# Powers of an exponential table computed directly, wider products, merged transfers and a halved inverse step in a DFT and long-convolution kernel

## The chip, the cores and the metric

The kernel runs on one core of one Trainium2 chip. The metric is the device time of one execution in microseconds (us). Lower is better.

## What is computed

Two independent parts whose results stand side by side in the output:

```python
# A: Fourier mixing, x is 2048 x 512
a = x @ dft_hid_re.T;  b = x @ dft_hid_im.T
ya = dft_seq_re @ a - dft_seq_im @ b
# B: diagonal state space layer as a long convolution, u is 2048 x 512, N = 128 states
dt = exp(log_dt);  A = -exp(log_A_real) + 1j * A_imag;  C = (C_real + 1j * C_imag) * dt
K[d, l] = 2 * real(sum_n C[d, n] * exp(A[d, n] * dt[d] * l))      # l = 0..2047
yb = irfft(rfft(u, 4096) * rfft(K, 4096))[:2048] + u * D_skip
out = concat(ya, yb)
```

All data are float32, and float32 accuracy is kept.

## The kernel before

The program is written by a planner (`Plan`): each piece of work is a generator that yields the engine it needs next and an assumed duration, and the planner, when the kernel is built, picks at each step the piece that can start first on its engine, with an urgency to break ties. What it picks is emitted at once. So each engine has a fixed order of instructions, and on the chip each engine takes its own in that order and waits wherever an operand isn't there.

**First part (`Fnet`).** Each product of two float32 tiles is three matmuls on a high and a low half (`hi`, `lo`). There are 12 groups: 8 named `("s", t, c)` with 16 row tiles each, 4 named `("p", t)` with 8. A row tile meets 4 column tiles `d`, so it gives 12 matmuls of 128 x 512, and the whole part gives 1920, all at L366. They are the *stream*, lowest in urgency, and fill TensorE wherever nothing else is ready. A row tile is loaded to `raw`, then split by one ScalarE copy to `hi` (L221) and one VectorE subtraction to `lo` (L225). Some pieces ("soft" ones) are split by two GpSimd transfers and one ScalarE copy instead. `evacuate` copies finished accumulators out; the last one (`d == 3` of the last group) is copied in two halves, by ScalarE (L382) and VectorE (L385).

**Second part (`Ssm`).** The kernel K is made from tables of powers. There are 16 blocks of 32 channels (`CHUNK`). For each block:

- `seed_args` (L636) makes the arguments of the powers 1, 2, 4, ..., 1024 of exp(A dt), 11 x 32 numbers for each row, and takes exponential, sine and cosine on ScalarE; `seeds` multiplies them to complex seeds `cs` (L675).
- `tables1` builds 32 outer powers `t1`, `tables2` 64 inner powers `t2`, by doubling: `mul` (L605) is a VectorE product with a seed, `add` (L614) combines real and imaginary parts, even powers come from squares (ScalarE L621, VectorE L628 and L634). Powers 3 and 5 to 7 of `t2` are two such products, of 128 and 384 elements for each row.
- `taps` (L801) sums over the states on TensorE: 64 calls of a 128 x 32 weight with 64 columns moving (float32 calls show as two matmuls each in the profile).

Every second block goes through `stage1_k` (L832), the first step of a Fourier transform in two steps; `stage1_u` (L890) is the same for u. Both go to DRAM and come back transposed. Then, for each quarter `h` of the channels and each of 4 parts `q`, `product` makes the second step for u and K (L992, 32 calls of 64 x 32 tiles with 256 columns), copies both out of PSUM on ScalarE (L1006), multiplies them on VectorE (L1009 to L1022), and makes the first inverse step with the matrix `ia` (L1029, 16 calls). The result is copied to `z` (L1044) and stored to `zs` in DRAM (L1053). When a quarter's four parts are stored, `inverse` runs twice for it: it loads half of `zs` as `zl` (L1073), makes the second inverse step with the matrix `ib` (L1078, 16 calls of a 128 x 64 weight with 128 columns moving), copies it out (two ScalarE copies, L1084) and stores 512 KB of the output (L1087).

The knobs that the change touches stand in these lines:

```python
LATE = 1, 1, 3, 1
...
CHUNK, FIRST, JOIN = 32, 128, 0
RAWS, DEPTH, STAGED, AHEAD = 7, 4, 4, 3
```

`LATE` is the urgency of a quarter's product copies, `RAWS` and `DEPTH` the numbers of buffers for `raw` and for `hi`/`lo`, `JOIN` the number of quarters whose first inverse step may share a TensorE block with `taps` (none).

## Time and profile before

| what | value |
|---|---|
| median of 3 runs | 583.82 us (583.13 to 583.96) |
| the profiled execution | 582.56 us |
| its span, first to last instruction | 580.8 us |
| TensorE (PE) matmuls busy | 571.1 us |
| VectorE (DVE) busy | 512.5 us |
| ScalarE (ACT) busy | 371.2 us |
| GpSimd (POOL) busy | 40.3 us |
| queue of SP, share of the 16 DMA engines' time | 66.7% |

The span is what the profile shows; the rest of an execution's time lies around it. "PEld" is TensorE's weight load, which overlaps the matmuls. Matmuls are pipelined: a stream matmul is listed with about 0.39 us, though the next one starts after 0.23, so what a run of them costs is read from starts, not from durations.

### The profile page before, as it was taken

What the parts mean: (1) busy time and instruction counts of PE and PEld (TensorE: products, weight loads), DVE (VectorE), ACT (ScalarE), POOL (GpSimd) and SP (SyncE); (2) the same over time, 40 slices, a digit from 0 to 9 for tenths busy, and PEclk for the clock granted to TensorE, in tenths of its full rate; (3) what the DMA queues carried; (4) which work ended last, traced back from release to release, by engine and by line L of the source; (5) the groups of instructions that cost most, each with busy time, mean ns of one, the idle gap of its engine ahead of it and who ended that gap; (6) DMA issues with size and microseconds to landing.
All of it is one profiled execution on the core that took longest, in us unless ns stands there. A gap on an engine that the chain in (4) does not pass through costs nothing.

```text
span 580.8 us, 15376 instructions
## 1 busy us (share of the span) xinstructions
PE 571.1 (98%) x6150; PEld 436.1 (75%) x6150; DVE 512.5 (88%) x911; ACT 371.2 (64%) x729; POOL 40.3 (7%) x60
## 2 busy tenths in 40 slices
PE   8999999999999999999999999999999999999996
PEld 6877777788777777778877777777687777776685
DVE  6999999999999999999999999999989999346410
ACT  4779665763777595768568585945588744445522
POOL 0000000000100000100000001001100000000000
PEclk9999999999999999999999999999999999999999
DMA  8999999986469767876797887479989995789564
GB/s 248 327 372 263 280 294 276 285 262 170 133 159 239 207 171 218 205 180 207 207 222 190 237 216 226 125 186 296 243 280 262 243 282 184 209 251 303 169 195 144
DMA packets 147831, 133.10 MB, mean 229 GB/s; under 512 B 47280, under 2 KB 107312, under 8 KB 147504
## 3 DMA queue, kind: packets, MB, share of 16 engines
q1 hardware_dynamic: 139408, 117.05, 66.7%
q0 software_dynamic: 8064, 14.68, 12.6%
q8 instruction: 48, 0.79, 0.6%
q10 hardware_dynamic: 288, 0.39, 0.2%
q14 instruction: 23, 0.19, 0.1%
HBM read 89.36 MB, written 42.73 MB: 227 GB/s over the span
## 4 chain that ended last, share of the span: by engine, by line
PE 70%; DVE 23%; issue 4%; DMA 2%; SPq 0%; ACT 0%; DVEq 0%; ACTq 0%
PE acc L366 55%; DVE prod L605 8%; DVE t L614 4%; PE f L992 4%; PE f L801 3%; DVE lo L225 3%; PE f L1029 3%; PE f L1078 2%; PE f L890 2%; DVE t L634 1%; PE f L832 1%; DVE z L1009 1%; DVE cs L675 1%; DMA zl<-zs 1%; DVE uk L1011 1%
## 5 line engine op out<-in xcount | busy, mean ns | idle before, releaser
L366 PE MATMUL acc<-hi,x_hi 128*128 128x512 f32 x640 | 258.2, 403 | 0.3 <-ACT hi L221 0.3
L366 PE MATMUL acc<-lo,x_hi 128*128 128x512 f32 x640 | 250.2, 391 | 0.0
L366 PE MATMUL acc<-hi,x_lo 128*128 128x512 f32 x640 | 249.7, 390 | 0.1
L605 DVE TENSOR_TENSOR prod<-t,cs 128x1024 f32<-128x1024 f32 (+4 forms) x192 | 163.1, 867 | 1.7 <-ACT t L723 0.6
L366 PEld LDWEIGHTS acc<-hi,x_hi 128*128 128x128 f32 x640 | 120.1, 188 | 49.8 <-issue 23.7
L366 PEld LDWEIGHTS acc<-hi,x_lo 128*128 128x128 f32 x640 | 120.3, 188 | 26.5 <-DVE x_lo L225 0.5
L366 PEld LDWEIGHTS acc<-lo,x_hi 128*128 128x128 f32 x640 | 120.3, 188 | 23.0 <-DVE lo L225 0.2
L221 ACT ACTIVATE hi<-raw 128x512 fp32r<-128x512 f32 x132 | 82.6, 627 | 64.0 <-PE acc L366 48.5
L225 DVE TENSOR_TENSOR lo<-raw,hi 128x512 fp32r<-128x512 f32 x132 | 90.1, 684 | 28.2 <-ACT hi L221 21.9
L614 DVE TENSOR_TENSOR t<-prod 128x512 f32<-128x512 f32 (+4 forms) x192 | 94.0, 511 | 1.0
L621 ACT ACTIVATE square<-t 128x256 f32<-128x256 f32 (+1 forms) x64 | 36.7, 573 | 31.0 <-DVE t L614 28.3
L320 POOL DMA_DIRECT2D lo<-in_sT x28 | 24.3, 868 | 214.1 <-ACT lo L318 33.8
L1006 ACT ACTIVATE uk<-f 128x1024 f32<-128x1024 f32 x32 | 31.1, 1017 | 11.8 <-PE f L992 11.8
L801 PEld LDWEIGHTS f<-t,t 128*32 128x32 f32 x2048 | 29.5, 110 | 7.9 <-issue 5.8
L801 PE MATMUL f<-t,t 128*32 128x64 f32 x2048 | 32.4, 220 | 1.9 <-issue 1.4
L389 ACT ACTIVATE y<-acc 128x512 f32<-128x512 f32 x47 | 28.0, 595 | 8.7 <-PE acc L366 8.6
L1009 DVE TENSOR_TENSOR z<-uk 128x512 f32<-128x512 f32 x32 | 21.9, 684 | 9.6 <-ACT uk L1006 7.4
L315 POOL DMA_DIRECT2D hi<-in_sT x28 | 16.2, 577 | 189.4 <-PE acc L366 147.0
L1044 ACT ACTIVATE z<-f 128x512 f32<-128x512 f32 x32 | 17.7, 592 | 13.3 <-PE f L1029 13.3
L634 DVE TENSOR_TENSOR t<-square 128x128 f32<-128x128 f32 (+1 forms) x64 | 24.6, 385 | 0.0
L992 PE MATMUL f<-xt,w 64*32 64x256 f32 x768 | 23.5, 379 | 0.0
L1011 DVE TENSOR_TENSOR uk<-uk 128x512 f32<-128x512 f32 x32 | 22.1, 690 | 0.9
(94 smaller groups left out, 490.7 us busy)
## 6 DMA issues: line engine op xcount, KB each, us to landing
raw<-in_sT SPq DMA_DIRECT2D x99, 256.0 KB, 5.4
p<-y SPq DMA_DIRECT2D x32, 256.0 KB, 3.2
xk<-xk_sb SPq DMA_DIRECT2D x32, 256.0 KB, 5.2
zs<-z SPq DMA_DIRECT2D x32, 256.0 KB, 3.3
zl<-zs SPq DMA_DIRECT2D x16, 512.0 KB, 5.0
raw<-p SPq DMA_DIRECT2D x32, 256.0 KB, 4.4
hi<-in_sT POOLq DMA_DIRECT2D x28, 256.0 KB, 4.6
lo<-in_sT POOLq DMA_DIRECT2D x28, 256.0 KB, 4.9
```

Source lines behind the costliest of these rows:

```text
L221: self.nc.scalar.activation(hi, src, AF.Copy)
L225: self.nc.vector.tensor_tensor(lo, src, hi.bitcast(F32), op=OP.subtract)
L366: nc.tensor.matmul(acc[d], l[:, cols], r, start=k == 0 and n == 0, stop=k == len(items) - 1 and n == 2)
L389: self.nc.scalar.activation(y, ps, AF.Copy, scale=-1.0 if g[2] == 1 else 1.0)
L605: self.nc.vector.tensor_tensor(p.rearrange("p k d c m -> p k (d c) m"), src.rearrange("p d c l -> p (d c) l")[:, None, :, rows].to_broadca ...
L614: self.nc.vector.tensor_tensor(dst[:, :, :, rows], p[:, 0], p[:, 1, :, ::-1], op=OP.add)
L621: self.nc.scalar.activation(sq, t[:, :, :, m // 2:m], AF.Square)
L634: self.nc.vector.tensor_tensor(t[:, :, 0, m:2 * m:2], box[0][:, :, 0], box[0][:, :, 1], op=OP.subtract)
L801: nc.tensor.matmul(ps[32 * j:32 * j + 32, i], t1[:, d, c], t2[:, d, c], start=c == 0, stop=c == 1, tile_position=(0, 32 * j))
L992: nc.tensor.matmul(got[r][1][32 * xx:32 * xx + 32, g, 256 * c:256 * c + 256], self.w2[rows, 2 * q + r, xx, 32 * c:32 * c + 32], xt[rows].r ...
L1006: a.activation(uk[:, r].rearrange("p g c n d -> p g (c n d)"), p, AF.Copy)
L1011: v.tensor_tensor(t[:, r], t[:, r], u[:, r, :, ::-1], op=OP.mult)
```

## The change

- **Powers 3, 5, 6, 7 directly.** The seed tile grows from 11 to 15 columns of 32. Four more ScalarE copies make 3, 5, 6 and 7 times the argument, and exponential, sine and cosine take them with the rest. One VectorE product of 256 elements makes a tile `ex` from them, and three ScalarE copies put it into `t2`. The two VectorE products and two sums that made these powers go.
- **Wide products.** For `h < 3` the two VectorE multiplications of a product run over both halves at once (1024 elements) after both ScalarE copies, not over each half (512) after its own.
- **Merged transfers.** The loads of `xt` and the store of `z` are one transfer where they were two (the tile of `h == 3` excepted, which lies in four buffers).
- **Halved second inverse step** for `h >= HALVED`, 2 (that is, 2 and 3): `inverse2`. The matrix `ia` gets a second version with another phase for `q >= 2`. `zl` is loaded as two halves of rows beside each other, one by SP's queue and one by GpSimd's; VectorE adds and subtracts them (two operations of 512 elements of each kind for each of the two `zl` tiles of a quarter); the step is then 32 calls of a 64 x 32 weight with 128 columns. The new matrix `ib2` is loaded after `zs` of `h == 1`.
- **Joining.** The second inverse step of `h < WAITS` (1), and what has waited, may share a TensorE block with `taps` or with a first inverse step (`late`).
- **The last copy** of the first part goes to two tiles, VectorE's first, and the stores of the last group are issued without a planned transfer slot.
- **The planner** gets 0.15 more slack ahead of TensorE, new durations for some pieces, `LATE = 3, 3, 3, 1`, `RAWS, DEPTH = 5, 5`; the set of soft pieces is written out, with the same members.

The core of the diff:

```diff
-LATE = 1, 1, 3, 1
+SLACK = 0.15
+LATE = 3, 3, 3, 1
...
                 if r[0] != p[5]:
-                    p[0] += HOP
+                    p[0] += HOP + (SLACK if r[0] == "pe" else 0.0)
...
         if g == self.groups[-1] and d == 3:
...
+            yield self.ys
+            y2 = self.pool.tile([128, DM], F32, name="y", bufs=STAGED)
+            yield "dve", dve(256)
+            self.nc.vector.tensor_copy(y2[:, 256:], ps[:, 256:])
             yield "act", act(256)
             self.nc.scalar.activation(y[:, :256], ps[:, :256], AF.Copy)
-            self.nc.sync.dma_start(out[:, :256], y[:, :256])
-            yield "dve", dve(256)
-            self.nc.vector.tensor_copy(y[:, 256:], ps[:, 256:])
-            self.nc.scalar.dma_start(out[:, 256:], y[:, 256:])
+            self.nc.sync.dma_start(out[:, 256:], y2[:, 256:])
+            self.nc.scalar.dma_start(out[:, :256], y[:, :256])
             return
...
-        s = self.tab.tile([128, 3, 11, CHUNK], F32, name="seed")
+        s = self.tab.tile([128, 3, 15, CHUNK], F32, name="seed")
...
+        for j, m in enumerate((3, 5, 6, 7)):
+            a.activation(args[:, :, j], args[:, :, 4], AF.Copy, scale=float(m))
...
+        ex = self.tab.tile([128, 2, 4, CHUNK], F32, name="ex", bufs=2)
+        yield "dve", dve(8 * CHUNK), *APART
+        self.nc.vector.tensor_tensor(ex, s[:, 1:3, :4], s[:, 0:1, :4].to_broadcast([128, 2, 4, CHUNK]), op=OP.mult)
...
-            p = yield from self.mul("prod2", t, slice(1, 2), cs[:, :, 1])
-            yield from self.add(p, t, slice(3, 4))
-            p = yield from self.mul("prod2", t, slice(1, 4), cs[:, :, 2])
-            yield from self.add(p, t, slice(5, 8))
+            ex = self.ex.pop(n)
+            yield "act", act(2 * CHUNK)
+            a.activation(t[:, :, :, 3].rearrange("p d c -> p c d"), ex[:, :, 0], AF.Copy)
+            for c in range(2):
+                yield "act", act(3 * CHUNK)
+                a.activation(t[:, :, c, 5:8].rearrange("p d j -> p j d"), ex[:, c, 1:], AF.Copy)
...
-            yield "dve", dve(512)
-            v.tensor_tensor(P[:, r], t[:, r], u[:, r], op=OP.mult)
-            yield "dve", dve(512), *APART
-            v.tensor_tensor(t[:, r], t[:, r], u[:, r, :, ::-1], op=OP.mult)
+            if h == 3:
+                yield from times(slice(r, r + 1), LAST)
...
         yield ready
+        if h < 3:
+            yield from times(slice(0, 2))
...
+    def inverse2(self, b, h, i, n):
+
+        nc, c = self.nc, n // 2
+        z = b.pool.tile([128, 2, c, PART], F32, name="zl", bufs=b.n)
+        view = self.zs[h].rearrange("(a s) c l d -> (s c) a l d", a=2)
+        yield "pool", ISSUE
+        for y, e in enumerate((nc.sync, nc.gpsimd)):
+            o = n * i + c * y
+            e.dma_start(z[64 * y:64 * y + 64], view[:, :, o:o + c])
+        yield "dma", load(64 * n, 270), FAST
+        t = b.pool.tile([128, c, PART], F32, name="zsum", bufs=b.n)
+        for w in range(0, c, 4):
+            m = slice(w, w + 4)
+            yield "dve", dve(512)
+            nc.vector.tensor_tensor(t[:, m], z[:, 0, m], z[:, 1, m], op=OP.add)
+            yield "dve", dve(512), *APART
+            nc.vector.tensor_tensor(z[:, 1, m], z[:, 0, m], z[:, 1, m], op=OP.subtract)
+        (k, ps), = yield from self.banks(1)
+        yield "pe", 1.06, None, 64
+        for o in range(0, c, 2):
+            for x in range(4):
+                for y in range(2):
+                    r, w = slice(64 * y, 64 * y + 64), o + x // 2
+                    nc.tensor.matmul(ps[32 * x:32 * x + 32, y, PART * (o // 2):PART * (o // 2) + PART],
+                                     self.ib2[r, c * i + w, x % 2], (t, z[:, 1])[x % 2][r, w], start=True, stop=True,
+                                     tile_position=(64 * y, 32 * x))
...
-RAWS, DEPTH, STAGED, AHEAD = 7, 4, 4, 3
+HALVED = 2
+RAWS, DEPTH, STAGED, AHEAD = 5, 5, 4, 3
+WAITS = 1
```

What the planner makes of it is read from the built order of both kernels. In the changed kernel the stream is L374, `taps` L833, the product L1025, the first inverse step L1069, the old second step L1172, the halved one L1145.

TensorE, the end of the program before: the second inverse steps of `h == 3` and the stream's last row tiles.

```order
L1078 MATMUL f1_7308<-zl_7272,ib_115 64x128 x16
L366 MATMUL acc_7191<-hi_7316,x_hi7_5770 128x512
L366 MATMUL acc_7191<-lo_7317,x_hi7_5770 128x512
L366 MATMUL acc_7191<-hi_7316,x_lo7_5771 128x512
L366 MATMUL acc_7220<-hi_7297,x_hi6_5733 128x512
L366 MATMUL acc_7220<-lo_7298,x_hi6_5733 128x512
L366 MATMUL acc_7220<-hi_7297,x_lo6_5734 128x512
L1078 MATMUL f0_7331<-zl_7273,ib_115 64x128 x16
L366 MATMUL acc_7220<-hi_7316,x_hi7_5770 128x512
L366 MATMUL acc_7220<-lo_7317,x_hi7_5770 128x512
```

After these rows 13 more stream matmuls follow, and the program ends with one. Now:

```order
L374 MATMUL acc_7205<-hi_7326,x_hi7_5650 128x512
L374 MATMUL acc_7205<-lo_7327,x_hi7_5650 128x512
L374 MATMUL acc_7205<-hi_7326,x_lo7_5651 128x512
L1145 MATMUL f1_7418<-zsum_7370,ib2_6657 32x128 x2
L1145 MATMUL f1_7418<-zl_7332,ib2_6657 32x128 x2
```

The first three rows are the last of the stream. Both halved steps of `h == 3`, 64 calls in all to `f1` and then `f0`, stand behind them, with 66 stream matmuls between the last first inverse step and them.

VectorE, the end of the program now (before, its last instruction is the copy L385, and only splits L225 stand ahead of it):

```order
L233 TENSOR_TENSOR lo_7288<-raw_7066,hi_7287 128x512
L233 TENSOR_TENSOR lo_7327<-raw_7083,hi_7326 128x512
L392 COPY y_7409<-acc_7205 128x256
L1136 TENSOR_TENSOR zsum_7370<-zl_7332 128x512
L1138 TENSOR_TENSOR zl_7332<-zl_7332 128x512
L1136 TENSOR_TENSOR zsum_7370<-zl_7332 128x512
L1138 TENSOR_TENSOR zl_7332<-zl_7332 128x512
```

The copy of the last accumulator `acc_7205`, which the stream's last matmul completes, stands ahead of the four operations of the first `zl` tile; four more, of `zl_7333`, follow.

VectorE, inside the tables, before (a block whose seeds are `cs_713`):

```order
L605 TENSOR_TENSOR prod2_1143<-t2_124,cs_713 128x128
L614 TENSOR_TENSOR t1_938<-prod_1126 128x32x16
L614 TENSOR_TENSOR t2_124<-prod2_1143 128x64
L605 TENSOR_TENSOR prod2_1173<-t2_124,cs_713 128x384
L225 TENSOR_TENSOR lo_1161<-raw_882,hi_1160 128x512
L902 TENSOR_TENSOR zl_249<-f0_1104,zl_249 128x512
L904 TENSOR_TENSOR zl_249<-f0_1104,zl_249 128x512
L614 TENSOR_TENSOR t2_124<-prod2_1173 128x64x3
```

and now the matching place of a block:

```order
L694 TENSOR_TENSOR cs_1442<-seed_1084 128x704
L699 TENSOR_TENSOR ex_1453<-seed_1084 128x256
L622 TENSOR_TENSOR prod_1451<-t1_1308,cs_1063 128x512
L233 TENSOR_TENSOR lo_1449<-raw_1366,hi_1448 128x512
L631 TENSOR_TENSOR t1_1308<-prod_1451 128x64x4
```

The four `prod2` instructions on `t2` are gone, and one product `ex` stands behind the seeds; the first `prod2` of a block is now the one of 512 elements. By the order, the stretch from the first `taps` to the last has 703 VectorE instructions before and 612 now.

## Rows read from the trace of the kernel before

**Rows 1.** The page: span, and busy us (share of the span) of two engines.
```profile
span 580.8 us, 15376 instructions
...
PE 571.1 (98%) x6150; PEld 436.1 (75%) x6150; DVE 512.5 (88%) x911; ACT 371.2 (64%) x729; POOL 40.3 (7%) x60
```

**Rows 2.** Windows: length, busy PE, PEld, DVE, ACT, POOL (instructions), granted clock, DMA share, GB/s.
```profile
83.00:488.40 405.40, 402.65 (x4780) 311.01 (x4780) 399.63 (x707) 274.67 (x549) 35.67 (x50) 1.00 0.80 220
488.40:576.00 87.60, 87.52 (x972) 65.82 (x971) 35.17 (x55) 37.07 (x60) 0.00 (x0) 1.00 0.70 208
576.00:580.80 4.80, 0.00 (x0) 0.00 (x0) 0.42 (x1) 0.34 (x1) 0.00 (x0) 0.90 0.50 176
```

**Rows 3.** The chain that ended last: start us, us, what, and how many instructions.
```profile
58.26 1.04 PE f L890 x16
...
77.33 1.91 PE f L890 x16
...
488.48 1.92 PE f L801 x128
490.40 2.26 PE acc L366 x9
492.67 1.05 PE f L1029 x32
...
508.82 1.90 PE f L1078 x32
...
516.38 1.89 PE f L992 x64
...
551.73 15.19 PE acc L366 x66
```

**Rows 4.** Timeline of TensorE inside one taps block: start, us, [idle before].
```profile
408.86 0.41 PE L801 MATMUL f<-t,t 128*32 128x64 f32 x10 [1.43 <-issue]
```

**Rows 5.** VectorE by line and shape (busy us, mean ns of one); then two starts from its timeline.
```profile
L605 DVE TENSOR_TENSOR prod<-t,cs 128x1024 f32<-128x1024 f32 x96 | 116.6, 1218 | 0.7
...
L605 DVE TENSOR_TENSOR prod<-t,cs 128x128 f32<-128x128 f32 x32 | 11.7, 377 | 0.6 <-ACT t L723 0.6
...
L605 DVE TENSOR_TENSOR prod<-t,cs 128x384 f32<-128x384 f32 x16 | 8.9, 554 | 0.1
...
L614 DVE TENSOR_TENSOR t<-prod 128x64 f32<-128x64 f32 x32 | 8.1, 271 | 0.1
...
L605 DVE TENSOR_TENSOR prod<-t,cs 128x256 f32<-128x256 f32 x16 | 6.7, 419 | 0.1
...
521.84 0.68 DVE L1019 TENSOR_TENSOR uk<-z 128x512 f32<-128x512 f32 x1
522.44 0.68 DVE L1022 TENSOR_TENSOR uk<-uk 128x512 f32<-128x512 f32 x1
```

**Rows 6.** Timeline of the end, and of one pair of output copies on ScalarE.
```profile
568.86 1.09 ACT L1084 ACTIVATE zl<-f 128x512 f32<-128x512 f32 x2 [7.39 <-PE f L1078]
...
575.53 0.39 PE L366 MATMUL acc<-hi,x_lo 128*128 128x512 f32 x1
575.96 0.38 ACT L382 ACTIVATE y<-acc 128x256 f32<-128x256 f32 x1 [0.76 <-PE acc L366]
...
576.37 0.42 DVE L385 COPY y<-acc 128x256 f32<-128x256 f32 x1 [14.18 <-ACT y L382]
...
576.83 0.36 ACTq L386 DMA_DIRECT2D out_ya<-y  x1
```

**Rows 7.** DMA issues of the last 15 us: KB each, median us to landing.
```profile
out_yb<-zl SPq DMA_DIRECT2D x2, 512.0 KB, 3.3
...
out_ya<-y ACTq DMA_DIRECT2D x1, 128.0 KB, 2.7
```

**Rows 8.** ScalarE by line and shape: busy us, mean ns of one.
```profile
L666 ACT ACTIVATE seed<-seed,halfpi 128x352 f32<-128x352 f32 x16 | 9.3, 578 | 0.0
...
L650 ACT ACTIVATE seed<-seed 128x64 f32<-128x64 f32 x16 | 4.1, 257 | 0.5
```

More of the change, by code (lines that the diff above doesn't have):

```diff
@@ L390, in evacuate @@
         self.plan.put(self.acc)
-        yield "dma", load(256)
+        if g != self.groups[-1]:
+            yield "dma", load(256)
         kind, t, c = g
@@ L414, in __init__, with run @@
         self.ssm, self.fn, self.got = ssm, run, None
[L416 to L420 removed]
+    def run(self, got, users, zone=0):
+        self.got, self.users, self.zone = got, users, zone
+        for k, _ in got:
+            users[k] = users.get(k, 0) + 1
+        self.fn(got, zone)
     def leave(self, k):
@@ L788, in taps @@
         other = self.waiting.pop(0) if self.waiting else None
-        got = yield from self.banks(2 if other else 1)
+        late = self.late.pop(0) if self.late and not other else None
+        got = yield from self.banks(2 if other or late else 1)
         k, p = got[0]
-        yield "pe", 1.97 + (1.05 if other else 0), None, 320 if other else 256
+        users = {k: 1}
+        yield "pe", 1.97 + (1.05 if other else IB if late else 0), None, 320 if other or late else 256
         if other:
-            other.run(got)
+            self.ia_done()
+        other = other or late
+        if other:
+            other.run(got, users)
         t1, t2 = self.t1.pop(n), self.t2
@@ L812, in taps @@
                              p[:, :, 256:].rearrange("p o (i l) -> p l o i", i=4), AF.Copy)
-        if other:
-            other.leave(k)
-        else:
+        users[k] -= 1
+        if not users[k]:
             self.give(k)
@@ L939, in take @@
                 yield self.sets[0].xts
-                xt = self.sets[0].pool.tile([128, 2, 4, 2, PART], F32, name="xt")
-                self.xt[h, q] = [[xt[:, r]] for r in range(2)]
+                xt = self.sets[0].pool.tile([128, 8, 2, PART], F32, name="xt")
+                self.xt[h, q] = [xt]
                 self.plan.set(self.take_ev[h, q])
@@ L961, in load_spectrum @@
         yield "dma", load(512, 270), FAST
-        for r in range(2):
-            for p, xt in enumerate(self.xt[h, q][r]):
-                n = xt.shape[1]
-                self.nc.sync.dma_start(xt[:, :, "uk".index(name)], view[2 * q + r, :, n * p:n * p + n])
+        for p, xt in enumerate(self.xt[h, q]):
+            n = xt.shape[1]
+            self.nc.sync.dma_start(xt[:, :, "uk".index(name)], view[q, :, n * p:n * p + n])
         self.plan.set(self.xt_ev[name, h, q])
@@ L1061, in inverses, with load_ib2 @@
         yield self.zs_ev[h]
-        b = self.sets[h // 3]
+        if h >= HALVED:
+            yield self.ib2_ev
+        b = self.sets[int(h >= min(HALVED, 3))]
         for i in range(2):
             yield b.zls
-            self.plan.spawn(self.inverse(b, h, i, 16), 1)
+            self.plan.spawn((self.inverse2 if h >= HALVED else self.inverse)(b, h, i, 16), 1)
+    def load_ib2(self):
+        yield self.set_ev[1]
+        yield self.zs_ev[1]
+        self.ib2 = self.sets[1].pool.tile([128, 16, 2, 32], F32, name="ib2")
+        yield "dma", load(512)
+        self.nc.sync.dma_start(self.ib2, self.ib2_in)
+        self.plan.set(self.ib2_ev)
@@ new lines, in inverse2 @@
+    def inverse2(self, b, h, i, n):
[15 more added lines that the diff above has]
+        (k, ps), = yield from self.banks(1)
+        yield "pe", 1.06, None, 64
+        for o in range(0, c, 2):
[5 more added lines that the diff above has]
+                                     tile_position=(64 * y, 32 * x))
+        for y in range(2):
+            yield "act", act(512)
+            nc.scalar.activation(z[:, 0, 4 * y:4 * y + 4].rearrange("p w d -> p (w d)"), ps[:, y], AF.Copy)
+        self.give(k)
+        yield "dma", load(32 * n, 270)
+        nc.sync.dma_start(self.out[:, c * i:c * i + c, PART * h:PART * h + PART], z[:, 0])
+        self.plan.put(b.zls)
```

149 lines of the change are left out of this document (96 added, 53 removed).

## Prediction

> **What bounds the kernel now.** I read the page's busy shares first: TensorE is busy 571.1 of 580.8 us and VectorE 512.5 [rows 1]. A busy TensorE is only a warning, so the windows by stage come next [rows 2]. There are three stages. From the first `taps` block (83.0 us) to the last (488.4 us) TensorE is busy 402.65 and VectorE 399.63 of 405.40 us: both are full. From there to 576 us TensorE alone is full (87.52 of 87.60), VectorE has 35 us of work. Then nothing runs on TensorE; ScalarE and VectorE copy one last tile and its stores land.
>
> The chain of waits gives the price of each piece of TensorE's order [rows 3]. A run of 66 stream matmuls lasts 15.19 us and one of 9 lasts 2.26: 0.227 us for each further matmul, and about 0.22 us of re-entry for each run. Blocks of the second part are 1.92 us (`taps`, L801), 1.89 (forward product, L992), 1.05 (first inverse step, L1029; I take the same for L832, also 16 calls with 256 columns), 1.90 (second inverse step, L1078) and 1.04 (stage 1 of u, L890, of which one took 1.91).
>
> With these prices TensorE's order between first and last taps should last 1356 × 0.227 + 15 × 1.92 + 12 × 1.89 + 18 × 1.05 + 4 × 1.90 + 2 × 1.04 + 50 × 0.23 = 399 us. It lasted 405.4, so 6.3 us are stalls; one of 1.43 us is shown as an issue gap inside a `taps` block [rows 4], the rest sits at blocks that wait for VectorE. Before 83.0 us I count another 1.9 us of the same kind, most in long L890 blocks.
>
> **The change, step by step.** Let T be the end of the last stream matmul, 575.92 us [rows 6]; 4.87 us follow it.
>
> *Work taken from TensorE ahead of T.* The order shows 1920 stream matmuls, 16 taps, 16 products, 16 first inverse steps, 8 of L832 and of L890 in both kernels. For h = 2 the two second inverse steps become 32 calls each, 64 rows by 32 columns with 128 columns moving, in place of 16 calls over 128 rows. No row has that shape. Bounds: 0.95 us, half of a product, which has the same tiles and twice the columns; 1.90 if nothing overlaps better. I take 1.05, nearest the product, with a fixed entry cost left in: 2 × 0.85 = **1.7 us** gained. For h = 3 both steps move behind the last stream matmul: 2 × 1.90 = **3.8 us** leave the stretch before T. Stream runs fall from 72 to 68: those two no longer cut the stream, and two more of the old second steps stand directly ahead of a taps block: 4 × 0.23 = **0.9 us**. Together T comes 6.4 us earlier at equal stalls.
>
> *VectorE in the table stage.* Each channel block loses four small instructions (128, 64, 384 and 192 elements), gets one of 256, and its seed row grows from 352 to 480 elements. In products of h < 3 two pairs of 512 become one pair of 1024. Durations are in [rows 5]; two independent 512-element operations that last 0.68 start 0.60 apart, so I take 0.07 off each. Between first and last taps the order has 64 fewer of 512 (39 us), 20 more of 1024 (23 us), 15 fewer of each of the small four (19 us together, the one of 192 put between 128x64 and 128x256), 13 more of 256 (4.5 us) and 24 longer seed operations (2 us). VectorE's 399.6 us become **371**. Part of it has only moved: taps now start at stream matmul 387, not 297, so more work of u and x lies ahead. TensorE's order for this stage, by the prices above, falls to 1266 × 0.227 + 15 × 1.92 + 11 × 1.89 + 17 × 1.05 + 4 × 1.90 + 44 × 0.23 = **372 us**. So VectorE stays as full as TensorE, where it was ahead by 0.6.
>
> *Stalls.* Two ends: 0 us in that stage if VectorE keeps a lead, and 5.3 if its old 5.8 us of idle time come on top of its 371. I take 3.9: the issue gap and its like stay (1.6), the waits for VectorE, 4.7 before, halve, because it no longer has more work than TensorE but has no more room either. Gain **2.4 us**. The 1.9 us ahead of the taps I leave.
>
> *ScalarE* gets four seed copies (0.257 each), three table copies in place of none (0.3 each, a guess from the same row for 64 to 96 numbers) and five wider seed functions (up to 0.14 each, by the slope between the two rows) per block [rows 8]: about 2.5 us, 37 us over the stage, where it was busy 275 of 405 [rows 2]. I cost this at nothing: the cover is the quarter of its time that stays idle. If it is gone, see the third rival.
>
> *Merged transfers* move the same bytes in 43 fewer SP issues; they lie beside TensorE's stream, and I cost them at nothing. Cover: matrix pieces wait split ahead of their use.
>
> *The tail.* This term loses. VectorE's order puts the last copy of the first part, which waits for T, ahead of the eight add and subtract operations of h = 3. Their data has landed by then (66 stream matmuls, 15 us, lie between the last first-step block and T), yet they can't start. So: copy 0.04 + 0.42 after T [rows 6]; eight operations at 0.61, 4.95; second block on TensorE 1.1; two ScalarE copies 1.09 [rows 6]; store of 512 KB 3.3 to landing [rows 7]; from the last landing (576.83 + 2.7) to the end of the span 1.27. Sum 12.25 after T, where 4.87 stood: **7.4 us lost**. Bounds: 7.0 with a block of 0.95 and a faster store; 9.3 with dependent operations (0.72 each) and a block of 1.90. The two last output halves no longer share a tile, which saves the copy's 0.4 us wait, but that wait isn't on this path any more.
>
> Sum: −6.4 − 2.4 + 7.4 = **−1.4 us**. The profiled execution took 582.56 us, 1.8 more than its span; the median of the runs is 583.82, so I forecast 582.4.
>
> *A clock that may speak against the tail.* TensorE is idle from T for 3.0 us, then for about 1.4 us between its two last blocks. In the kernel before, the granted clock was 0.90 over the last 4.80 us [rows 2]: it went from 2.4 to 1.2 GHz about 3.8 us after the last matmul. Both gaps are shorter, so the sum uses the full clock; no row shows such a gap with work behind it. The Trainium skill, page "TensorE: Matmul & The Clock Gate", section "HAM oscillation — how this bites in real kernels", says that waits between groups of matmuls put TensorE back to its low clock, group after group; by that the fourth rival would be the case.
>
> **Rivals.**
> 1. *VectorE's relief is real.* If its lead at the first taps lasts, stalls in the stage fall from 6.3 to about 0.1: −6.4 − 6.2 + 7.4 = −5.2, 578.6 us. For: 91 fewer instructions and every removed one was on a dependent chain. Against: 371 beside 372.
> 2. *The tail eats the gain.* The stalls stay at 6.3: −6.4 + 7.4 = +1.0, 584.8; at the tail's upper bound +2.9, 586.7. It decides as soon as the stalls fall by less than 1.0 us. For: VectorE's order at the end is fixed, the eight operations can't pass the copy. Against: only that stalls should fall a little. This one ends slower than before. That the halved step halves nothing (blocks of 1.90) would end there too: 1.7 us for h = 2 and 0.85 in the tail come back, +1.2, 585.0.
> 3. *ScalarE becomes what VectorE waits for.* It rises from 68% to about 80% of the stage, and each block's seeds pass through it between VectorE steps. If VectorE's idle time there goes from 5.8 to 10, the stage lasts 381 and its stalls are 9: −6.4 + 2.7 + 7.4 = +3.7, 587.5. Against: seeds are made a block ahead.
> 4. *The clock falls in the tail.* All as forecast, but the last block runs at 1.2 GHz: 1.05 more, −0.3, 583.5. For: two idle gaps in a row. Against: each is shorter than the 3.8 us after which it fell before.
>
> **Chances.** Forecast (−2.6 to −0.2 us) 0.40, rival 1 0.20, rival 2 0.21, rival 3 0.14, rival 4 0.05. A measurement of this kernel tells about 0.2%, 1.2 us, from no change. Faster by more: rival 1 and 0.24 of the forecast, 0.44. Within: 0.16 of the forecast, 0.10 of rival 2 and rival 4, 0.31. Slower: 0.11 of rival 2 and rival 3, 0.25. The range leaves out the lower third of rival 1 and the upper half of rival 3: 578.4 to 587.4. The likeliest case alone spans 581.2 to 583.6.
>
> **What would show it.** In the windows by stage: first to last taps near 376 us, VectorE busy near 371. At the end: last stream matmul near 567 us, VectorE's copy, then eight operations without a gap, two blocks of about 1 us each, last store issued about 7.7 us after T, end 12.3 after T. I am wrong if the stage lasts 372 or 381 (rivals 1 and 3), if the eight operations run ahead of T, or if the blocks last 1.9.

## The result, and the profile after

| | before | changed |
|---|---|---|
| median of 20 executions each | 583.05 us (580.98 to 584.28) | 585.68 us (583.54 to 588.83) |
| the profiled execution, its span | 582.56, 580.8 us | 584.1, 582.2 us |

The ratio is 1.0050, interval 1.0037 to 1.0063: slower by 2.6 us in the medians, where 1.4 us of gain was forecast. By the profiled spans it is 1.4 us slower. The changed kernel's times also spread more, so differences of 1 or 2 us between single profiles of its kind carry little: in four profiles of nearly its order (its own, and those of three runs below) T lies between 570.45 and 573.35, and its own is the earliest.

The busy line of the changed kernel's page answers to [rows 1]: VectorE loses 1.6 us, ScalarE gains 24, which is 1.5 us for each of 16 blocks.

```profile
span 582.2 us, 15626 instructions
...
PE 567.7 (98%) x6278; PEld 432.1 (74%) x6278; DVE 510.9 (88%) x855; ACT 395.1 (68%) x841; POOL 42.7 (7%) x64
```

The windows by stage of the changed kernel answer to [rows 2], cut at its own first taps (107.0), last taps (485.4) and T (570.45); the columns are the same.

```profile
107.00:485.40 378.40, 374.44 (x4566) 291.44 (x4568) 369.94 (x612) 276.74 (x614) 32.81 (x46) 1.00 0.79 213
485.40:570.45 85.05, 85.05 (x1068) 62.31 (x1067) 41.91 (x64) 38.18 (x60) 2.42 (x4) 1.00 0.87 233
570.45:582.20 11.75, 4.16 (x128) 2.18 (x128) 5.59 (x9) 2.56 (x5) 0.00 (x0) 0.83 0.61 182
```

| | before | forecast | changed |
|---|---|---|---|
| first to last taps | 405.4 | 376 | 378.4 |
| of it stalls (length less the priced order) | 6.0 | 3.9 | 5.9 |
| T | 575.92 | 567 | 570.45 |
| T to the end | 4.87 | 12.25 | 11.78 |

The prediction's prices, as printed, add up to 399.4 us for the order before (not 399) and to 372.5 now; so the stalls were 6.0 us, not 6.3, and are 5.9.

So the tail is as forecast, VectorE's 369.9 us in the stage are as forecast (371), and T comes 3.3 us too late. 2.2 of these are the stalls of the table stage, which fell by 0.2 us at most where 2.4 was forecast. What TensorE waited for has changed, though. Its waits before, between first and last taps:

```profile
PE f L801 <- issue: 1.4, 1, 1.4
PE f L832 <- DVE ks L824: 0.6, 1, 0.6
PE f L801 <- DVE t L614: 0.4, 1, 0.4
```

The waits of TensorE in the changed kernel:

```profile
PE f L833 <- issue: 1.2, 1, 1.2
PE f L1145 <- DVE zsum L1136: 1.2, 1, 1.2
PE f L1172 <- ACT uk L1039: 1.2, 1, 1.2
...
PE acc L374 <- ACT y L399: 0.7, 1, 0.7
...
PE f L1025 <- DVE xk_sb L877: 0.2, 1, 0.2
...
PE f L833 <- DVE z L935: 0.2, 1, 0.2
```

In the table stage the waits put down to VectorE go from 1.0 us to 0.4 (L1145 is the tail); waits for ScalarE, 1.2 and 0.7, stand there now. The prediction had put 4.7 us of waits down to VectorE; these views name only 1.0. That VectorE held the stage by about 5 us is shown by the run with its relief alone, below. Of the chain that ended last, the shares by engine say the same. Before:

```profile
PE 70%; DVE 23%; issue 4%; DMA 2%; SPq 0%; ACT 0%; DVEq 0%; ACTq 0%
```

Changed:

```profile
PE 67%; DVE 19%; ACT 6%; issue 5%; DMA 3%; SPq 0%; ACTq 0%; DVEq 0%
```

ScalarE was no part of that chain; now 6% of the span hang on it. The end of the changed kernel, from its timeline, answers to [rows 6]:

```profile
570.48 0.42 DVE L392 COPY y<-acc 128x256 f32<-128x256 f32 x1 [12.24 <-PE acc L374]
570.83 0.68 DVE L1136 TENSOR_TENSOR zsum<-zl 128x512 f32<-128x512 f32 x1
571.54 0.69 DVE L1138 TENSOR_TENSOR zl<-zl 128x512 f32<-128x512 f32 x1
...
571.65 0.41 PE L1145 MATMUL f<-zsum,ib 64*32 64x128 f32 x4 [1.21 <-DVE zsum L1136]
...
574.36 1.09 ACT L1150 ACTIVATE zl<-f 128x512 f32<-128x512 f32 x2 [1.21 <-PE f L1145]
575.47 3.04 SPq L1153 DMA_DIRECT2D out_yb<-zl  x2
...
575.52 0.69 DVE L1138 TENSOR_TENSOR zl<-zl 128x512 f32<-128x512 f32 x1
...
577.01 1.08 ACT L1150 ACTIVATE zl<-f 128x512 f32<-128x512 f32 x2 [1.57 <-PE f L1145]
```

VectorE's copy waits 12.24 us for T with the eight operations behind it, as the prediction said; they end at 576.2, the last copy at 578.1, the span at 582.2. TensorE starts each part of a block as soon as its own operand is there.

### The profile page after: what moved, and what is told of

It is laid out like the page before. It is cut to its first block, busy times and chain, and to the rows that moved or that the text cites. A ratio compares the mean times of both kernels' runs of the same rounds, so it can differ in the third digit from the quotient of the medians.

```text
span 582.2 us, 15626 instructions
## 1 busy us (share of the span) xinstructions
PE 567.7 (98%) x6278; PEld 432.1 (74%) x6278; DVE 510.9 (88%) x855; ACT 395.1 (68%) x841; POOL 42.7 (7%) x64
## 4 chain that ended last, share of the span: by engine, by line
PE 67%; DVE 19%; ACT 6%; issue 5%; DMA 3%; SPq 0%; ACTq 0%; DVEq 0%
PE acc L374 52%; DVE prod L622 7%; PE f L1025 5%; PE f L833 4%; DVE t L631 4%; PE f L1069 3%; DVE lo L233 2%; PE f L1172 1%; DMA xt<-xk 1%; DMA xk<-xk_sb 1%; ACT L679 1%; DVE t L651 1%; PE f L863 1%; DVE zl L933 1%; ACT hi L229 1%
## 5 line engine op out<-in xcount | busy, mean ns | idle before, releaser
L374 PE MATMUL acc<-hi,x_hi 128*128 128x512 f32 x640 | 257.7, 403 | 1.3 <-ACT y L399 0.7
L374 PE MATMUL acc<-lo,x_hi 128*128 128x512 f32 x640 | 250.2, 391 | 0.5 <-DMA lo<-in_sT 0.5
L374 PE MATMUL acc<-hi,x_lo 128*128 128x512 f32 x640 | 249.6, 390 | 0.1
L374 PEld LDWEIGHTS acc<-hi,x_hi 128*128 128x128 f32 x640 | 120.1, 188 | 50.5 <-issue 22.5
L622 DVE TENSOR_TENSOR prod<-t,cs 128x1024 f32<-128x1024 f32 (+3 forms) x160 | 150.6, 949 | 2.7 <-ACT t L776 1.6
L374 PEld LDWEIGHTS acc<-hi,x_lo 128*128 128x128 f32 x640 | 120.2, 188 | 26.4 <-DVE x_lo L233 0.5
L374 PEld LDWEIGHTS acc<-lo,x_hi 128*128 128x128 f32 x640 | 120.2, 188 | 24.4 <-DMA lo<-in_sT 1.3
L631 DVE TENSOR_TENSOR t<-prod 128x512 f32<-128x512 f32 (+3 forms) x160 | 86.8, 551 | 1.0
L833 PEld LDWEIGHTS f<-t,t 128*32 128x32 f32 x2048 | 29.4, 110 | 6.7 <-issue 5.1
L833 PE MATMUL f<-t,t 128*32 128x64 f32 x2048 | 32.1, 220 | 1.4 <-issue 1.2
L843 ACT ACTIVATE ks<-f 128x512 f32<-128x512 f32 x16 | 9.5, 596 | 32.3 <-PE f L833 32.3
L1050 DVE TENSOR_TENSOR z<-uk 128x1024 f32<-128x1024 f32 (+1 forms) x20 | 20.1, 1006 | 5.7 <-ACT uk L1039 5.7
L1025 PE MATMUL f<-xt,w 64*32 64x256 f32 x768 | 23.7, 379 | 0.5 <-DVE xk_sb L877 0.2
```

The lines of the kernel that those rows point to most:

```text
L374: nc.tensor.matmul(acc[d], l[:, cols], r, start=k == 0 and n == 0, stop=k == len(items) - 1 and n == 2)
L622: self.nc.vector.tensor_tensor(p.rearrange("p k d c m -> p k (d c) m"), src.rearrange("p d c l -> p (d c) l")[:, None, :, rows].to_broadca ...
L631: self.nc.vector.tensor_tensor(dst[:, :, :, rows], p[:, 0], p[:, 1, :, ::-1], op=OP.add)
L833: nc.tensor.matmul(ps[32 * j:32 * j + 32, i], t1[:, d, c], t2[:, d, c], start=c == 0, stop=c == 1, tile_position=(0, 32 * j))
L1025: nc.tensor.matmul(got[r][1][32 * xx:32 * xx + 32, g, 256 * c:256 * c + 256], self.w2[rows, 2 * q + r, xx, 32 * c:32 * c + 32], xt[rows].r ...
```

## The experiments

My theory after the result: the direct powers relieve VectorE, which pays, and load ScalarE, which costs more than nothing. Rivals: the new order holds the time, or the halved step at the end does. "Ratio" is to the kernel before, with its interval in brackets.

**The end.** First the halving undone:

```diff
-        self.plan.spawn(self.load_ib2(), 1)
-HALVED = 2
+HALVED = 4
```

> The changed kernel with the old second inverse step for all quarters (the halved step and its matrix load taken out; all else as changed; the order differs only in the last twelfth of the stream). Theory A, the tail costs the gain: the profiled execution of the changed kernel ends 11.8 us after its last stream matmul (570.4 to 582.2) where 4.9 us stood before; with the steps back inside the stream that matmul comes about 6.0 us later (two steps of 1.9 with a re-entry each, and twice 0.85 for h = 2), and the tail falls to about 4.5: 1.3 us faster than the changed kernel, about 581 us span, ratio to the kernel before 1.000 to 1.003. Theory B, the stalls of the table stage or the merged transfers are the loss: as slow as the changed kernel, ratio 1.004 to 1.006.

584.16 us, ratio to before 1.0029 (1.0011 to 1.0047). In its profile T is 575.91 and the tail 5.11: the halving brings T 5.46 us forward and lengthens the tail by 6.67. By these two profiles it loses about 1.2 us; the intervals of the two kernels overlap (the changed one's begins at 1.0037), so the executions alone don't show the loss. The rest of the change is still not faster than before: without the halving T is where it was (575.92).

The last copy on ScalarE, so that VectorE's eight operations may run ahead of T:

```diff
-            yield "dve", dve(256)
-            self.nc.vector.tensor_copy(y2[:, 256:], ps[:, 256:])
+            yield "act", act(256)
+            self.nc.scalar.activation(y2[:, 256:], ps[:, 256:], AF.Copy)
```

> The changed kernel with the last copy of the first part made by ScalarE alone, so that nothing on VectorE stands between the data of h = 3 and its eight add and subtract operations; TensorE's order is the same. Theory A with VectorE's order as the cause: the first tile's four operations run ahead of the last stream matmul; the second tile's data landed 1.7 us after that matmul, so its operations end about 4.4 us after it, not 5.8: tail 10.4 in place of 11.8, 1.4 us faster than the changed kernel, ratio 1.002 to 1.004. Rival, the landing of the data is what ends last: no gain (ratio 1.004 to 1.006). In either case the stage of the tables should be as in the changed kernel, 378 us.

584.55 us, 1.0038 (1.0019 to 1.0056), an interval that overlaps the changed kernel's; the tail is 10.23 us, as expected. Four of the eight operations now start by T, but the second tile's data is late. VectorE's timeline there:

```profile
571.80 0.69 DVE L1138 TENSOR_TENSOR zl<-zl 128x512 f32<-128x512 f32 x1
574.02 0.69 DVE L1136 TENSOR_TENSOR zsum<-zl 128x512 f32<-128x512 f32 x1 [1.53 <-DMA zl<-zs]
```

The next run halves for `h == 2` alone, with the old step inside the stream for `h == 3` (in `product` and the choice of `inverse2`):

```diff
-        if h >= HALVED:
+        if h == HALVED:
...
-        yield "dma", load(64 * n, 270), FAST
+        yield "dma", load(64 * n, 270 if h < 3 else 400), FAST
```

> The changed kernel with the halved step for h = 2 alone; h = 3 takes the old step, planned inside the stream (both steps stand ahead of the last 6 and 3 stream matmuls). Theory A: the last stream matmul about 4.3 us later than in the changed kernel (574.7), the tail about 5 us: span 579.7, 2.5 us faster than the changed kernel and about 1 us faster than the kernel before, ratio 0.997 to 1.000. Theory B: ratio 1.003 or more.

585.84 us, 1.0054 (1.0033 to 1.0075): not faster, as theory B had it. The tail is 5.99 as meant, but the stage took 382.2 us in its profile, the slowest of its six executions, with TensorE's waits of 1.0 to 1.2 us spread over five places; the end alone doesn't decide. Next the ScalarE copy again, with both halves of `zl` on SP's queue (`for y, e in enumerate((nc.sync, nc.sync))`):

> As e2, and both halves of each zl tile loaded by SP's queue, none by GpSimd's. In the changed kernel the four loads of h = 3, issued from 559.8 to 561.5, landed at 565.3, 567.8, 571.5 and 572.1, the GpSimd ones after 7.5 and 11 us; before, the same bytes landed within 8.2 us. If GpSimd's queue is slow: all landed by about 568, all eight operations done by the last stream matmul, tail about 8 us (two blocks of 1.1, copies 1.1, store 3.3, 1.3 to the end): 2.4 us faster than e2. If transfers of 64 partitions are slow by themselves, whichever queue issues them: as e2.

585.74 us, 1.0057 (1.0036 to 1.0078). The loads take as long from one queue (see the last section), and VectorE waits 2.07 us for the second tile. In this run the clock fell in the tail (see rival 4 below).

**ScalarE and VectorE by themselves.** Four runs that keep every engine's order. In the changed kernel, six of the seven new ScalarE copies of a block left out (powers 3 and 5 to 7 set to zero):

```diff
-        for j, m in enumerate((3, 5, 6, 7)):
-            a.activation(args[:, :, j], args[:, :, 4], AF.Copy, scale=float(m))
+        a.activation(args[:, :, 0:4], args[:, :, 4:8], AF.Copy)
...
-            a.activation(t[:, :, :, 3].rearrange("p d c -> p c d"), ex[:, :, 0], AF.Copy)
...
-                a.activation(t[:, :, c, 5:8].rearrange("p d j -> p j d"), ex[:, c, 1:], AF.Copy)
```

> The changed kernel with less work on ScalarE and the same order otherwise: one copy where four made 3, 5, 6 and 7 times the argument, and none of the three copies of the tile of extra powers (those powers are not computed). About 1.6 us of ScalarE less per block, 25 us in all. Theory S, in the table stage ScalarE took VectorE's place as what TensorE waits for (in the changed kernel's trace TensorE waits 1.2 us for a copy of a product and 0.7 for an accumulator's copy, none over 0.2 for VectorE): the stage shortens from 378 to 382 us to about 375, the run by 3 us or more, ratio to the kernel before 0.997 to 1.000. Rival I, the stalls are instruction fetch and chance, whatever ScalarE does: no difference, ratio 1.004 to 1.006.

584.36 us, 1.0024 (1.0011 to 1.0038); ScalarE busy 383.3, 12 us less, not the 25 expected. This is between the two readings: the 3 us of theory S did not come, the stage in its profile is no shorter (379.8 us), and the interval touches the changed kernel's. Then the seven made twice:

> The changed kernel with those seven ScalarE copies per block issued twice, the same order otherwise: about 1.8 us more ScalarE per block, 29 us in all. Theory S: the stage lengthens by 4 us or more, ratio 1.011 or more. Rival I: within 1 us of the changed kernel, ratio 1.004 to 1.008.

594.78 us, 1.0198 (1.0179 to 1.0218), ScalarE busy 418.8. So 24 us more on ScalarE cost 9 us, and 12 us less gave back 1.3 at most: past the changed kernel's load the cover is gone. That ScalarE's load is what holds the stalls left in the changed kernel itself is not shown by these two: TensorE's longest wait for ScalarE there, 1.2 us at L1172, is 1.1 in both.

In the kernel before, the four small VectorE operations of a block left out (the powers 3 and 5 to 7 aren't computed):

```diff
-            p = yield from self.mul("prod2", t, slice(1, 2), cs[:, :, 1])
-            yield from self.add(p, t, slice(3, 4))
-            p = yield from self.mul("prod2", t, slice(1, 4), cs[:, :, 2])
-            yield from self.add(p, t, slice(5, 8))
+            for n_el in (128, 64, 384, 192):
+                yield "dve", dve(n_el)
```

> The kernel before without the four small VectorE operations per block that the change removes (powers 3 and 5 to 7 are not computed), with the same order otherwise: what VectorE's relief alone is worth, 1.27 us per block, 20 us in all, with nothing added to ScalarE. If VectorE was what held the stage (my prediction's reading: 399.6 us busy of 405.4): VectorE 380 us, the stage falls from 405.4 to about 400 us, 4 to 6 us faster, ratio 0.990 to 0.993. If TensorE's own stalls held it: within 1.5 us, ratio 0.997 to 1.001.

576.99 us, 0.9895 (0.9879 to 0.9911): 14 us less on VectorE give 6. Its stage from first to last taps (columns as in [rows 2]) and its chain's shares show where the limit is then:

```profile
82.69:483.11 400.42, 400.28 (x4780) 310.44 (x4780) 386.77 (x648) 273.31 (x549) 35.56 (x50) 1.00 0.81 223
...
PE 98%; DMA 1%; issue 0%; ACT 0%; DVE 0%; SPq 0%; DVEq 0%
```

TensorE has the same order as before and is idle for 0.14 us of this stage. So the order without stalls takes 400.3 us, the stalls before were 5 us, and VectorE's relief removes them all.

And in the kernel before, nine copies more for each block on ScalarE (the three of L743 and L746, each four times):

> The kernel before with nine ScalarE copies per block more (each of the three copies of powers 1, 2 and 4 made four times), 2.3 us per block, about as much as the change adds, with the same order otherwise and VectorE as before: what ScalarE's load alone costs. Theory S: 3 us or more slower, ratio 1.005 or more. My prediction costed it at nothing: ratio 0.998 to 1.002.

606.82 us, 1.0406 (1.0371 to 1.0440): ScalarE busy 413.2 where it was 371.2, and 42 us of load cost 24. Its share of the chain goes from 0% to 11%:

```profile
PE 52%; DVE 27%; ACT 11%; issue 6%; DMA 3%; SPq 1%; DVEq 0%; ACTq 0%
```

The added copies stand ahead of their block's VectorE products, so the time alone doesn't tell ScalarE's load from a longer way through a block. VectorE's waits in the stage speak for both:

```profile
DVE prod L605 <- ACT t L723: 8.5, 4, 3.1
...
DVE prod L605 <- ACT t L746: 2.4, 3, 1.2
DVE prod L605 <- ACT t L752: 2.0, 3, 1.2
```

L746 and L752 are among the multiplied copies; L723 is not, and VectorE waited 0.6 us for it before.

**The direct powers alone.** The diff's parts in `seed_args`, `seeds` and `tables2` put into the kernel before, planned anew with the old settings:

> The kernel before with the direct powers alone (15 seed columns, the product ex, seven more ScalarE copies a block), planned anew; old products, old transfers, old second steps, old buffers, old LATE. If VectorE's relief is paid for on ScalarE (the relief alone gave 6 us with nothing put on ScalarE), the stage of the tables keeps stalls of 4 to 8 us and the time is within 0.6% of the kernel before, 580 to 586. If ScalarE's extra work is free, as I cost it, the stalls fall to 1 to 3 us and the time is 577 to 580. If the two other parts of the change (wide products, urgencies and buffers) were what lost the relief, this run is near 578 too, so those two readings are told apart by the next two runs.

596.94 us, 1.0246 (1.0219 to 1.0274), far outside what either reading gave. In the profile the stage's stalls are 5.6 us by the same prices, but the planner ended the order with first inverse steps of the last quarter behind T, and the load of `zl` after them is bare. TensorE's timeline at that end:

```profile
573.64 0.39 PE L366 MATMUL acc<-hi,x_lo 128*128 128x512 f32 x1
573.96 1.12 PE L1039 MATMUL f<-uk,ia 32*64 32x256 f32 x32
584.68 6.50 PE L1088 MATMUL f<-zl,ib 128*64 128x128 f32 x64 [9.60 <-DMA zl<-zs]
```

So this run and the three next to it tell of the planner's order first. The three copies into `t2` on GpSimd (`nc.gpsimd.tensor_copy`), then also the four scaled arguments (`nc.gpsimd.tensor_scalar`), then both in the changed kernel without halving:

> As the run before, but the three copies into t2 for each block are made by GpSimd instead of ScalarE (0.9 us a block off ScalarE). If ScalarE's load is the price: 1 to 3 us faster than the run before. If its place in the chain is what counts and GpSimd copies are slower than ScalarE's 0.3 us, it is the same or slower, and VectorE's squares wait for GpSimd.

> As the run before, and the four scaled arguments come from GpSimd as well (another 1.0 us a block off ScalarE; what stays on ScalarE is 0.6 us a block of wider functions). If ScalarE's load is the price: 578 to 581, 0.99 to 0.997 of the kernel before. If GpSimd is slow at these or holds up VectorE beside it, no faster than the run before last.

> The changed kernel with old second steps (no halving) and with the seven copies of a block on GpSimd, planned anew. The changed kernel without the halving took 584.2. If ScalarE's load is the price: 579 to 582. If not: 584 again. If wide products and five buffers are worth something beside, it beats the run before; if they cost, it loses to it.

602.55 us, 1.0350 (1.0332 to 1.0369); 594.61, 1.0218 (1.0197 to 1.0238); 598.19, 1.0288 (1.0266 to 1.0309). None gave the gain that the reading by load asked for, and all have new orders again (in the first two 34 and 24 us lie behind T), so the load on ScalarE can't be read from them. GpSimd is slow at it, by the second run's rows:

```profile
L653 POOL TENSOR_SCALAR seed<-seed 128x64 f32<-128x64 f32 x64 | 45.6, 713 | 73.4 <-ACT seed L648 69.6 <-issue 0.7
```

Hence the same powers in the old order. The diff is that of the first run of this part, with the planner still given the old pieces (the four VectorE yields, no yields for the new copies), so that TensorE's, SP's and GpSimd's rows are those of before one by one:

> The kernel before with the change's direct powers and nothing else, every engine's order kept (the four VectorE operations of a block left out, one product, the seven ScalarE copies and the wider functions put in their places). VectorE's relief alone gave 577.0 and 2.3 us a block more on ScalarE alone cost 24 us. If ScalarE's load is the price: 580 to 592, with TensorE's or VectorE's waits for ScalarE. If the new order is what lost the relief: 576.5 to 579, as with the relief alone.

587.64 us, 1.0078 (1.0062 to 1.0095): 5 us slower than before, 10.6 slower than with the relief alone, with no change of order. This is the run that tells the direct powers from the new order. Its chain:

```profile
PE 56%; DVE 17%; ACT 12%; DMA 7%; issue 7%; SPq 1%; POOL 0%; DVEq 0%; ACTq 0%; POOLq 0%
```

and its stage from first to last taps, where VectorE has 6 us less than before [rows 2] and ScalarE 20 more:

```profile
86.07:493.31 407.24, 403.10 (x4781) 310.52 (x4781) 393.32 (x661) 294.73 (x643) 35.57 (x50) 1.00 0.80 219
```

Of the 4.9 us by which T comes later than before (580.82 against 575.92), 3.1 lie ahead of the first taps (86.07 against 83.0) and only 1.8 in the stage. What takes the 3.1 us, no run isolates.

Then the load taken back in steps. Powers 1 to 7 side by side in `ex`, `cs` of 8 columns, the table filled by two copies:

```diff
+        ex = self.tab.tile([128, 2, 7, CHUNK], F32, name="ex", bufs=2)
+        self.nc.vector.tensor_tensor(ex, s[:, 1:3, :7], s[:, 0:1, :7].to_broadcast([128, 2, 7, CHUNK]), op=OP.mult)
...
+            for c in range(2):
+                a.activation(t[:, :, c, 1:8].rearrange("p d j -> p j d"), ex[:, c], AF.Copy)
```

> As the run before, with less on ScalarE for the same powers: all seven powers 1 to 7 lie side by side in the product, so two copies of 224 numbers fill the table in place of six, cs shrinks from 11 to 8 columns, and 9 copies make the arguments. By the rows of the two kernels ScalarE gets about 1 us a block more than before the change instead of 2.5. If load is the price: 3 to 8 us faster than the run before. If not, the same.

587.51 us, 1.0085 (1.0070 to 1.0099): no gain, because the load didn't fall. ScalarE is busy 392.4 us, not the 387 I had counted on (371.2 and 1 us a block). The two wide copies are dear, by its rows:

```profile
L752 ACT ACTIVATE t<-ex 128x224 f32<-128x224 f32 x32 | 16.6, 623 | 0.0
```

1.25 us for both, where two of 373 and four of 313 to 317 ns in the run before took 2.0 in all and overlapped; and the arguments are nine copies in both runs. Then the arguments by one GpSimd product of 960 numbers:

> As the run before, with all 15 arguments of a block made by one GpSimd product of 960 numbers instead of 9 ScalarE copies: ScalarE then has about 1.4 us a block less than before the change. If load is the price: 575 to 578, the fastest kernel of the study. If GpSimd needs 5 us or more for it, or makes it late behind a transfer that waits on its queue, the seeds are late: 580 or more.

609.99 us, 1.0477 (1.0452 to 1.0502): the other side of what was expected. The product took 2.83 us (busy, mean ns, idle before), and ScalarE waited for it:

```profile
L651 POOL TENSOR_TENSOR seed<-par,times 128x960 f32<-128x960 f32 x12 | 34.0, 2829 | 17.4 <-DMA par<-par_dram 14.0 <-issue 3.4
...
ACT seed L654 <- POOL seed L651: 26.6, 12, 4.9
```

VectorE was held up beside it. It is busy 532.0 us with 863 instructions, where the run before has 506.6 with as many; the longer ones lie beside the product. From the timeline:

```profile
117.26 3.07 POOL L651 TENSOR_TENSOR seed<-par,times 128x960 f32<-128x960 f32 x1 [3.40 <-issue]
...
118.69 2.71 DVE L608 TENSOR_TENSOR prod<-t,cs 128x1024 f32<-128x1024 f32 x1
```

Such a VectorE product takes 1.22 us elsewhere [rows 5]; here it ends 1.07 us after GpSimd's does. So this run, too, doesn't tell what less load on ScalarE is worth.

The lean tables in the changed kernel without halving:

> The changed kernel without the halving (584.2) and with the lean tables of the second run, in its own order: 1.4 us a block less on ScalarE than the changed kernel. The changed kernel gave back 1.3 to 1.5 us when six of seven copies were left out, so by load 582 to 583.5; if the order is what holds it, 584 again.

583.04 us, 1.0016 (1.0001 to 1.0031). The time is inside what was expected, but ScalarE's busy time fell by 3 us only, and the interval overlaps that of the kernel without halving: not told. At last the two copies on VectorE (`nc.vector.tensor_copy`), in the old order and in the changed kernel's:

> The lean tables in the order of the kernel before, with the two copies into the table for each block made by VectorE instead of ScalarE (they were 0.62 us each on ScalarE). ScalarE's busy time should be near that of the kernel before, 371 to 378 us, and VectorE's 8 to 12 us less than before (relief 14, copies back 4 to 6). If both loads count as the runs so far say (VectorE's relief of 14 us gave 5 to 6, ScalarE's 25 more took 10): 578 to 581. If it is the length of the chain through ScalarE and back, not its load: 576 to 578. If something else in the direct powers costs the time: 586 or more, as the two runs before it.

> The same exchange in the order of the changed kernel without the halving and with lean tables (583.0): ScalarE 15 us or so less busy, VectorE 5 or so more. By load: 580 to 582.5, as there too TensorE's waits named ScalarE. If VectorE is the tighter one in that order: 584 to 586.

593.83 us, 1.0181 (1.0164 to 1.0199), and 593.17, 1.0183 (1.0156 to 1.0210). Again my price was off: the copies take VectorE 15.3 us, not the 4 to 6 counted on, so it ends with more work than before the change.

```profile
L755 DVE COPY t<-ex 128x224 f32<-128x224 f32 x32 | 15.3, 563 | 0.0
```

The row is from the old order, where ScalarE then waits for those copies ahead of its squares, 23.4 us in all. The runs in the old order together (busy time within the stage from first to last taps, us):

| kernel | first taps | VectorE busy | ScalarE busy | stage | median of the executions |
|---|---|---|---|---|---|
| VectorE's relief alone | 82.7 | 386.8 | 273.3 | 400.4 | 577.0 |
| before | 83.0 | 399.6 | 274.7 | 405.4 | 583 |
| direct powers | 86.1 | 393.3 | 294.7 | 407.2 | 587.6 |
| direct powers, lean | 86.2 | 393.3 | 292.1 | 407.4 | 587.5 |
| lean, copies on VectorE | 86.7 | 403.6 | 280.6 | 412.4 | 593.8 |
| before, ScalarE loaded | 84.7 | 400.5 | 313.9 | 426.7 | 606.8 |

ScalarE is full in none of these rows, and work put on either engine moves the time. Each row also changes who waits for whom inside a block, so busy time and place are not told apart by it. No version beat the kernel before: what would is the first row, and a way to the four powers that loads neither engine was not found.

## Why the prediction was wrong

- **The step that failed** is "I cost this at nothing: the cover is the quarter of its time that stays idle", and with it "the waits for VectorE ... halve". The direct powers in the old order cost 5 us; VectorE's relief alone gives 6. In the stage itself the relief takes 5.0 us off and the direct powers put 1.8 on; the rest of their price, 3.1 us, falls ahead of the first taps, where the prediction forecast no change. The idle quarter of ScalarE is no cover. As I read it, that is because much of it is ScalarE waiting for TensorE or VectorE, as in these waits before:

```profile
ACT hi L221 <- PE acc L366: 48.5, 38, 3.2
ACT square L621 <- DVE t L614: 28.3, 25, 3.0
```

  Why each us on it costs about half a us (24 for 42) I read as one chain that passes from engine to engine, each in fixed order; the chain's shares (0%, 11%, 12%) show ScalarE in it, but the passing itself was not isolated.
- **ScalarE's size** was off the safe way: 2.5 us a block summed from durations, 1.5 in busy time (24 us in 16 blocks), since its short copies overlap. Even so it cost more than the relief gave: the product `ex` and the wider seeds give VectorE back 8 of its 14 us (506.5 busy against 498.3).
- **Stalls**: 5.9 us, forecast 3.9. The waits that the profile names changed, and the size stayed. In numbers this is rival 2 (stalls unchanged, 584.8); of rival 3's mechanism (ScalarE is waited for) a part is seen, as VectorE's idle time in the stage went from 5.8 to 8.5 us, where rival 3 had 10. What holds the 5.9 us in the new order was not isolated. With stalls that fell by 0.2 us and not 2.4, and 1.1 us more elsewhere (TensorE is idle for 2.9 us ahead of the first taps, 2.05 before), T came 3.3 us late; that alone turns the sign.
- **Work ahead of T**: 1.7 + 3.8 = 5.5 us for the halving; undoing it moves T by 5.46. The size is right, the close match in part luck: by the prediction's prices the undoing also brings back two re-entries, which makes 6.0, and single profiles differ by more than that. The 0.9 for re-entries was not tested alone, nor were wide products and merged transfers. All the change's parts without halving (1.0029) do better than its powers in the old order (1.0078), so something in the rest, or in its new order, gives back about 0.5%; which part wasn't tried.
- **The tail**: 11.78 against 12.25. Right, though "their data has landed by then" held for the first tile only: the second landed at 572.1, 1.7 us after T, and only the copy and the first tile's operations ahead hid it; the runs with the copy on ScalarE show it.
- **The clock** (rival 4): the windows of the changed kernel's end show the granted clock full while TensorE has gaps of 1.2 us and less, and low behind its last matmul.

```profile
571.35:578.00 6.65, 4.16 (x128) 2.18 (x128) 4.73 (x8) 2.46 (x5) 0.00 (x0) 1.00 0.65 205
578.00:582.20 4.20, 0.00 (x0) 0.00 (x0) 0.00 (x0) 0.10 (x1) 0.00 (x0) 0.53 0.50 141
```

  Rival 4 did not happen in this kernel, and its premise was wrong for it: the idle gaps forecast as 3.0 and 1.4 us are this short because TensorE starts at each operand, not after all four. But the prediction's reason against rival 4, that gaps shorter than 3.8 us are safe, doesn't hold. Here the clock fell about 1.3 us after the last matmul (estimated from the 0.53). In the run with the ScalarE copy and both halves on SP's queue it fell inside the tail, after a wait of 1.64 us, and the last block ran at 1.2 GHz:

```profile
574.40:576.00 1.60, 0.04 (x3) 0.00 (x0) 0.73 (x2) 0.12 (x1) 0.00 (x0) 1.00 1.05 390
576.00:577.20 1.20, 0.90 (x32) 0.56 (x32) 1.20 (x2) 0.69 (x2) 0.00 (x0) 0.97 0.50 174
577.20:579.20 2.00, 1.85 (x44) 0.82 (x32) 0.75 (x2) 0.65 (x2) 0.00 (x0) 0.50 0.40 118
```

  A longer gap with work behind it is in the run with the direct powers alone, planned anew: after its wait of 9.60 us the two second steps took 6.50 us, where the prediction's price for two is 3.80.

```profile
584.60:588.00 3.40, 3.32 (x32) 3.35 (x34) 0.00 (x0) 0.00 (x0) 0.00 (x0) 0.50 0.93 361
588.00:591.20 3.20, 3.18 (x36) 2.94 (x32) 0.00 (x0) 1.08 (x2) 0.00 (x0) 0.62 0.25 69
```

  By the Trainium skill's page "TensorE: Matmul & The Clock Gate", section "HAM oscillation — how this bites in real kernels", waits for loads between groups of matmuls bring the low clock back. The trace of that run agrees, with 0.50 behind its wait for `zl`; the tail of the changed kernel, with 1.00 over the whole of 571.35 to 578.00, has no wait for a load.

## What to carry to other kernels

An engine that was idle for a quarter of a stage was no cover here, where its work lies inside the loop that the full engines wait for; before work is moved to such an engine, price it by a run that adds that load in the same order, and look ahead of the stage too. Test such a change in the old order as well as planned anew: the new order alone moved the kernel with direct powers by 9 us (596.94 against 587.64), and it was its tail that grew. And count a relief net of what the replacement puts on the same engine.

## What the hardware showed that I had not expected

The halved step's loads, two half tiles of 64 rows each, were much slower than the old ones of 128 rows with the same 512 KB. DMA issues of the last 33 us of the changed kernel (KB each, median us to landing):

```profile
zl<-zs SPq DMA_DIRECT2D x2, 512.0 KB, 8.3
zl<-zs POOLq DMA_DIRECT2D x2, 512.0 KB, 9.3
```

With both halves on SP's queue (the fourth run):

```profile
zl<-zs SPq DMA_DIRECT2D x4, 512.0 KB, 8.0
```

Before, with 128 rows:

```profile
zl<-zs SPq DMA_DIRECT2D x4, 512.0 KB, 5.5
```

So GpSimd's queue isn't the reason. While they ran, the changed kernel's DMA engines were busy all the time at little more than half the rate; its window, and then that of before:

```profile
563.00:569.00 6.00, 6.00 (x28) 4.95 (x27) 0.00 (x0) 1.20 (x2) 0.00 (x0) 1.00 1.03 215
```

```profile
559.00:562.00 3.00, 3.00 (x15) 2.45 (x14) 1.02 (x2) 0.63 (x1) 0.00 (x0) 1.00 1.00 381
```

Share 1.03 at 215 GB/s, against 1.00 at 381. That the 64 rows are the reason is likely and was not isolated. The other surprises stand above: copies into the table of 224 numbers a row take 0.62 us on ScalarE and 0.56 on VectorE, and GpSimd takes 0.71 us for 64 numbers a row, where ScalarE takes 0.24.
